# Softmax: the row scale is taken from the probabilities to the attention output, and s is loaded first

## The chip, the cores and the metric

One core of a Trainium2 chip runs the whole program. Its engines work side by side, each through its own list of instructions in a fixed order: TensorE (PE; PEld is its weight load), VectorE (DVE), ScalarE (ACT), GpSimd (POOL), and SyncE (SP), whose queue issues every DMA here. An instruction waits on semaphores of the others, and whatever stands behind it on its engine waits with it. The metric is the device time of one execution in microseconds (us).

## What is computed

```
# 64 heads (8 batches x 8), 576 tokens, 64 columns a head
scores = q @ k.T / 8 - (cum[i] - cum[j])      # cum = cumsum(max(s, 0)), causal
attn = exp(scores - rowmax)
attn = attn / (sum(attn, -1) + 1e-9)
x = attn @ v                                  # 8 heads side by side: 576 x 512 a batch
# then, for each batch, a gated MLP with a token mixing
h = gelu(x @ w_in); u, v = halves of h
v_n = (v - mean) / sqrt(var + 1e-6) * g_ln
out = x + (u * (w_sg @ v_n + b_sg)) @ w_out
```

All of it is in float32; most matrix products are made of two or three products of parts (a high part in float32r and the rest).

## The kernel before, in words

**Attention.** A head goes through three generators. `scores(h)` forms the scores of the 576 rows in five row tiles `it` (64, 128, 128, 128 and 128 rows; because of the causal mask they need 64, 192, 320, 448 and 576 columns). On DVE, `ttr` takes them out of PSUM, adds the mask, and writes them to `pbuf[h % 2][it]` with a running minimum of the negated score in `mn`. `exp_` makes the exponential on ACT in place and leaves the row sums in `sums`. `norm` then takes the reciprocal of the sums (`rs`, one value a row) and multiplies the probabilities by it, in seven pieces, six of them in place or nearly so on POOL for a head below 12 (the 448 columns of tile 3 go to ACT there) and all seven on POOL for the others. Three of the pieces also carry a 64 x 64 block into a free corner of another tile, so that a transpose later takes two blocks in one go. `transposes(h)` transposes `pbuf` on PE into PSUM tiles `pt`, which ACT and DVE take out; `pv(h)` multiplies by v into `xx` and a small tile `x` (`x0` in the code), and ACT and DVE add the result into `xr`, one tile of 128 x 576 for a pair of heads: partitions are the columns of x, the free axis is the tokens.

**Heads.** The first 8 heads load k and q (`kf`, `qf`) as they are; the others load `raw`, split it on ACT and POOL (`k<-raw`), and move the parts into place by five DMAs on SP, of which `k<-k` and `k<-cum` are the last two. Before head 0, the cumulative sums of s are made: load of `st`, three steps on DVE, a product with a triangle `tri` on PE (`cps`), `cf`, and the rows `kf<-cf`. Eight products `wm` that nobody reads keep PE busy until head 0's scores.

**MLP.** `ffn(b)` begins by splitting the four `xr` tiles of a batch on POOL into `xs`, and then runs units v, u, s and o (PE tiles `vm`, `um`, `sm`, `om`). A weight is loaded once, split by ACT, DVE and POOL (`wraw`, `wbits`, `wi`, `wo`, `ws`) during the first 14 heads or so. Tiles of one tag share a ring of buffers; the ring `gt` holds the gated halves that o units read, and the staging of weights in the beginning; the ring `u2` holds u, the outputs `ot` and other small things.

**What sets the order.** The program is recorded as a list of operations, each with a key (its place in a nominal time line of one head a step); `plan` goes through them by a table of costs, takes for each engine the ready operation that can start first, and by key among those, and fixes each engine's order; `emit` writes it out. All lines of the profile therefore name the line of `emit` that issues, L283, and the tiles tell the operations apart. Of the names in the profile, the buffer numbers are left out: `p` is any tile of `pbuf`, `mn` the minima, `k` any tile of k or its parts, `q` likewise.

Of the kernel before, what the change touches and what calls it, by code (L numbers as in the profile page):

```python
# [21 lines left out]
P = 128  # L22
# [3 lines left out]
CH = S // 2  # L26
# [7 lines left out]

TOK = [0, 1, 2, 5, 6, 8, 7, 4, 3]
IT0 = [0, 64, 448, 192, 320]
ITR = [64, 128, 128, 128, 128]
# [11 lines left out]
NP = 12  # L49
U2 = 7  # L50
ENG = {'k': 'sg', 'vs': 'sg', 'xs': 'gg', 'ln': 'sg', 'gt': 'sg', 'w': 'gg', 'ws': 'sv', 'n': 'ggggg', 'n0': 'gggsg', 'ws1': 'g'}
MT = 52.0
# [36 lines left out]
class View:  # L89
# [330 lines left out]
def tile_attn_gmlp(  # L420
# [91 lines left out]
    for i in range(WARM):  # L512
# [14 lines left out]
                            compare_op=ALU.is_ge, fill=NEG)  # L527
    mask2 = const.tile([P, S], BF16, name="mask2")
    nc.vector.memset(mask2, 0.0)
    for r0, c in ((0, 512), (64, 448)):  # L530
        nc.gpsimd.affine_select(out=mask2[r0:r0 + 64, :], in_=mask2[r0:r0 + 64, :], pattern=[[-1, S]], base=c,
                                channel_multiplier=1, compare_op=ALU.is_ge, fill=NEG)
# [8 lines left out]
    for i in range(2):  # L541
        t = const.tile([66, S], F32R, name=f"q2_{i}")
        nc.vector.memset(t[64:66, :].bitcast(F32), 1.0)
        q2.append(t)
        ts_ = []
        for it in range(5):
            t = const.tile([P, PW[it]], F32, name=f"p_{i}_{it}")
            if PW[it] > ITW[it]:
                nc.gpsimd.memset(t[:, ITW[it]:PW[it]], 0.0)
            ts_.append(t)  # L550
        pbuf.append(ts_)
        t = const.tile([P, 5], F32, name=f"sum_{i}")
        nc.vector.memset(t, 1.0)
        sums.append(t)
# [10 lines left out]
    def part(wide, src, hi, lo):  # L565
        n = 256
        if not wide:
            t = moe.tile([P, 2, CH], F32, name="wst", tag="gt", bufs=5)
            t = t.rearrange("p a n -> p (a n)")[:, 0:n]
            nc.sync.dma_start(out=t, in_=src)  # L570
            split(hi, lo, t, nc.scalar, nc.gpsimd)
            return
        raw = moe.tile([P, CH, 2], I32, name="wraw", tag="gt", bufs=5)
        with later():
# [23 lines left out]
    def w_sg_part():  # L598
# [10 lines left out]
        for f in range(2):  # L609
# [7 lines left out]
            t = moe.tile([P, CH], F32, name="wst", tag="u2", bufs=U2)  # L617
            bh = moe.tile([1, 2, CH], F32R, name="bh", tag="gt", bufs=5)
            nc.sync.dma_start(out=t[0:1, :], in_=b_sg.rearrange("(o t) -> o t", o=1)[:, fs])
# [43 lines left out]
    def ttr(h, it, pst, c0, j0, j1, first):  # L663
        d = heads[h]
        r = ITR[it]
        m0 = (576 if it in (2, 4) else 448) - ITW[it] if it else 320
        mn = d["mn"]
        nc.vector.tensor_tensor_reduce(
            out=pbuf[h % 2][it][0:r, j0:j1], in0=pst[0:r, c0:c0 + j1 - j0],
            in1=(mask2 if it in (2, 4) else mask)[0:r, m0 + j0:m0 + j1], scale=-0.125,  # L670
            scalar=3.0e38 if first else mn[0:r, it:it + 1],
            op0=ALU.add, op1=ALU.min, accum_out=mn[0:r, it:it + 1])

    def exp_(h, it):
        d = heads[h]
        r, w = ITR[it], ITW[it]
        p = pbuf[h % 2][it][0:r, 0:w]
        nc.scalar.activation(out=p, in_=p, func=AF.Exp, bias=d["mn"][0:r, it:it + 1], scale=-1.0,
                             accum_out=sums[h % 2][0:r, it:it + 1])

    def norm(h, its, rs):
        c = slice(min(its), max(its) + 1)
        nc.scalar.activation(out=rs[:, c], in_=sums[h % 2][:, c], func=AF.Copy, bias=1e-9)
        nc.vector.reciprocal(out=rs[:, c], in_=rs[:, c])
        for it in its:
            r, w = ITR[it], ITW[it]
            p = pbuf[h % 2][it][0:r, 0:w]
            e = eng("n0" if h < NP else "n")[it]


            o = [(p, p, rs[0:r, it:it + 1])]
            if it == 0:
                o = [(pbuf[h % 2][3][0:64, 384:448], p, rs[0:64, 0:1])]
            elif it == 1:
                o = [(p[:, 0:P], p[:, 0:P], rs[:, 1:2]),
                     (pbuf[h % 2][2][64:P, 256:320], p[64:P, P:192], rs[64:P, 1:2])]
            elif it == 4:
                o = [(p[:, 0:512], p[:, 0:512], rs[:, 4:5]),
                     (pbuf[h % 2][3][0:64, 448:512], p[0:64, 512:S], rs[0:64, 4:5])]
            for po, pi, f in o:  # L700
                if e is nc.scalar:
                    nc.scalar.activation(out=po, in_=pi, func=AF.Copy, scale=f)
                else:
                    e.tensor_scalar(out=po, in0=pi, scalar1=f, scalar2=1.0, op0=ALU.mult, op1=ALU.mult)

    def scores(h):
# [25 lines left out]
        yield 0.6  # L732
        rs = att.tile([P, 5], F32, name="rs", tag="rs")
        norm(h, (3, 0, 2, 1, 4), rs)
        yield 0.1
# [62 lines left out]
    def pv(h):  # L798
# [40 lines left out]
        hs = slice(64 * half, 64 * half + 64)  # L839
        for ps, o, sl in ((x0, slice(0, 64), slice(0, 64)), (xx, slice(0, 512), slice(64, S))):  # L840
            if f32:
                nc.scalar.copy(out=xt[hs, sl], in_=ps[0:64, o])
            else:
                nc.scalar.copy(out=xt[hs, sl], in_=ps[64:128, o])
                nc.vector.tensor_tensor(out=xt[hs, sl], in0=ps[0:64, o], in1=xt[hs, sl], op=ALU.add)
        del heads[h]
        yield 0.5


    def ffn(b):  # L850
# [24 lines left out]
        def v_unit(tt, _):  # L875
# [33 lines left out]
            gelu2(ps[0:r], t, ps[0:r])  # L909
            bs = moe.tile([P, 6], F32, name="bs", tag="bs", bufs=2)  # L910
            mv = moe.tile([P, 2], F32, name="mv", tag="mv", bufs=2)
            rt = moe.tile([P, 4], F32, name="rt", tag="rt", bufs=2)
            nc.vector.bn_stats(out=bs[0:r], in_=ps[0:r])
# [42 lines left out]
        def s_unit(ch, dt):  # L956
# [141 lines left out]
```

## Time and profile before

| | |
|---|---|
| time, median of 3 runs | 835.5 us (834.99 to 836.14) |
| profiled execution, first to last instruction | 835.4 us, no other time of it is given |
| instructions | 16823 |
| busy: PE, PEld | 795.3 us (95%), 688.4 us (82%) |
| busy: DVE, ACT, POOL | 607.0 us (73%), 581.9 us (70%), 607.3 us (73%) |
| DMA | 69805 packets, 89.30 MB, 107 GB/s over the span |
| mean granted clock of TensorE | 0.994 |

The program starts with the load of s and the cumulative sums (to about 12 us), goes on with the first 12 heads, beside which the weights are loaded and split (to about 160 us), then runs attention of one batch beside the MLP of the one before (to about 760 us), and ends with the MLP of the last batch. A row of grouped instructions reads: engine, operation, out<-in tiles, shape, xcount, then busy us and mean ns of one, then the engine's idle time just before them and what ended it. A row of waits reads: who waited for whom, us in total, times, longest.

### The profile page before, as it was taken

What the parts mean: (1) busy time and instruction counts of PE and PEld (TensorE: products, weight loads), DVE (VectorE), ACT (ScalarE), POOL (GpSimd) and SP (SyncE); (2) the same over time, 40 slices, a digit from 0 to 9 for tenths busy, and PEclk for the clock granted to TensorE, in tenths of its full rate; (3) what the DMA queues carried; (4) which work ended last, traced back from release to release, by engine and by line L of the source; (5) the groups of instructions that cost most, each with busy time, mean ns of one, the idle gap of its engine ahead of it and who ended that gap; (6) DMA issues with size and microseconds to landing.
All of it is one profiled execution on the core that took longest, in us unless ns stands there. A gap on an engine that the chain in (4) does not pass through costs nothing.

```text
span 835.4 us, 16823 instructions
## 1 busy us (share of the span) xinstructions
PE 795.3 (95%) x5097; PEld 688.4 (82%) x5097; DVE 607.0 (73%) x1846; ACT 581.9 (70%) x1620; POOL 607.3 (73%) x1043
## 2 busy tenths in 40 slices
PE   5989888999999999999999999999999999999998
PEld 3445555899888999889988989889988999889998
DVE  4677687866788667986789667886679767984562
ACT  3677787676778577985788666976679766883350
POOL 3786979578587976978677967769769885866351
PEclk9999999999999999999999999999999999999999
DMA  5555653325443444335543435244534354320101
GB/s 184 160 172 168 160 129 96 97 75 148 114 102 84 119 124 118 92 87 136 127 108 74 119 106 146 54 112 119 132 82 108 92 139 117 94 46 22 49 7 57
DMA packets 69805, 89.30 MB, mean 107 GB/s; under 512 B 25954, under 2 KB 42212, under 8 KB 69716
## 3 DMA queue, kind: packets, MB, share of 16 engines
q1 hardware_dynamic: 69716, 88.23, 40.2%
q8 instruction: 41, 0.67, 0.4%
q14 instruction: 48, 0.39, 0.2%
HBM read 42.27 MB, written 9.73 MB: 62 GB/s over the span
## 4 chain that ended last, share of the span: by engine, by line
PE 75%; DVE 7%; ACT 6%; POOL 6%; DMA 2%; issue 2%; SPq 0%; POOLq 0%; DVEq 0%; ACTq 0%
PE sm L283 13%; PE om L283 12%; PE xx L283 11%; PE sc L283 10%; PE vm L283 10%; PE pt L283 9%; PE um L283 9%; POOL p L283 3%; ACT p L283 2%; DVE p L283 1%; DMA raw<-in_kq 1%; DVE vt L283 1%; DVE u L283 1%; PE x L283 1%; ACT xr L283 1%
## 5 line engine op out<-in xcount | busy, mean ns | idle before, releaser
L283 POOL TENSOR_SCALAR p<-p,rs 128x512 f32<-128x512 f32 (+3 forms) x436 | 194.5, 457 | 37.7 <-DVE rs L283 22.5
L283 ACT ACTIVATE p<-p,mn 128x448 f32<-128x448 f32 (+4 forms) x320 | 177.8, 557 | 37.2 <-DVE mn L283 35.7
L283 PE MATMUL pt<-ident,p 128*128 128x128 f32 x768 | 154.4, 283 | 10.5 <-POOL p L283 5.0
L283 DVE CUSTOM_DVE_ANT_0 p<-sc,mask 128x448 f32<-128x448 f32 (+4 forms) x320 | 124.6, 419 | 32.8 <-PE sc L283 23.8
L283 PE MATMUL sc<-k,q 66*128 66x288 f32 (+9 forms) x672 | 142.2, 313 | 4.0 <-DVE mn L283 2.0
L283 PE MATMUL um<-xs,wi 128*128 128x288 f32 x768 | 135.6, 305 | 3.1 <-DVE vt L283 2.3
L283 PE MATMUL sm<-ws,vn 128*128 128x288 f32 x768 | 135.5, 305 | 1.2 <-DVE u L283 1.0
L283 PE MATMUL om<-gt,wo 128*128 128x288 f32 x768 | 132.4, 301 | 0.0
L283 PEld LDWEIGHTS pt<-ident,p 128*128 128x128 f32 x768 | 95.5, 141 | 39.7 <-POOL p L283 12.2
L283 PE MATMUL vm<-wi,xs 128*128 128x512 f32 (+1 forms) x416 | 124.6, 407 | 0.0
L283 PEld LDWEIGHTS um<-xs,wi 128*128 128x128 f32 x768 | 113.0, 190 | 7.0 <-DVE vt L283 4.1
L283 PEld LDWEIGHTS sm<-ws,vn 128*128 128x128 f32 x768 | 112.9, 190 | 4.3 <-DVE u L283 3.5
L283 PEld LDWEIGHTS sc<-k,q 128*128 128x128 f32 (+3 forms) x672 | 102.3, 183 | 16.1 <-DVE mn L283 4.5
L283 PEld LDWEIGHTS om<-gt,wo 128*128 128x128 f32 x768 | 112.3, 189 | 2.1 <-POOL gt L283 0.2
L283 POOL TENSOR_TENSOR k<-raw,k 128x576 fp32r<-128x576 f32 x56 | 80.2, 1432 | 36.2 <-ACT k L283 36.2
L283 PEld LDWEIGHTS vm<-wi,xs 128*128 128x128 f32 (+1 forms) x416 | 72.8, 185 | 11.4 <-POOL xs L283 0.2
L283 POOL TENSOR_TENSOR gt<-u,gt 128x288 fp32r<-128x288 f32 x64 | 50.6, 805 | 32.3 <-ACT gt L283 32.1
L283 POOL TENSOR_TENSOR vs<-vr,vs 128x384 fp32r<-128x384 f32 x52 | 52.6, 1011 | 27.5 <-ACT vs L283 26.0
L283 DVE SCALAR_TENSOR_TENSOR u<-u,um 128x288 f32<-128x288 f32 x128 | 56.4, 443 | 14.3 <-ACT u L283 13.4
L283 DVE TENSOR_TENSOR pbl<-pt,pbh 128x512 fp32r<-128x512 f32 x104 | 56.6, 549 | 8.8 <-ACT pbh L283 8.4
L283 ACT CAST pbh<-pt 128x512 fp32r<-128x512 f32 x104 | 49.5, 481 | 17.1 <-PE pt L283 16.8
L283 ACT ACTIVATION_READ_ACCUMULATOR p<-p,mn 128x1 f32 (+1 forms) x320 | 60.4, 189 | 0.0
(122 smaller groups left out, 1547.0 us busy)
## 6 DMA issues: line engine op xcount, KB each, us to landing
q<-k SPq DMA_DIRECT2D x168, 144.0 KB
raw<-in_kq SPq DMA_DIRECT2D x56, 288.0 KB
vr<-in_vp SPq DMA_DIRECT2D x52, 192.0 KB
out_t<-ot SPq DMA_DIRECT2D x64, 144.0 KB
k<-k SPq DMA_DIRECT2D x56, 144.0 KB
wraw<-in_w_in SPq DMA_DIRECT2D x16, 256.0 KB
kf<-in_kq SPq DMA_DIRECT2D x8, 288.0 KB
qf<-in_kq SPq DMA_DIRECT2D x8, 288.0 KB
```

The source lines that it names most:

```text
L283: r = getattr(op["eng"].real, op["name"])(*[f(a) for a in op["args"]], **{k: f(v) for k, v in op["kw"].items()})
```

## The change

`norm` goes, and with it the multiplication of the probabilities. The transposes take the bare exponentials. Two pieces that `norm` had moved while it scaled them are now plain copies of 64 x 64 on POOL (the 64 x 64 tile 0 is exponentiated by ACT right into its corner of tile 3, out of another corner of the same tile, where DVE puts it). The row scale is needed along the free axis now, since `xr` has the tokens there: the reciprocals `rs`, 128 x 5, go to a row `rd` in memory, one element of 4 bytes at a time, and are read back into 64 partitions at once (`rb`, 64 x 576 for each head of a pair). After the second head of a pair, POOL multiplies `xr` by `rb`, 128 x 576. So that `rd` is in the order of the tokens in `xr`, the order of the token blocks changes (`TOK`, `IT0`, and `COL`, the column of the sums). `rb` has one buffer; to make room for it the mask is cut to what is used and the ring `gt` goes from 5 buffers to 4, while `u2` goes from 7 to 8. The operations of the beginning get the key -5, ahead of all loads.

```diff
-TOK = [0, 1, 2, 5, 6, 8, 7, 4, 3]
-IT0 = [0, 64, 448, 192, 320]
+TOK = [1, 2, 5, 6, 8, 7, 4, 3, 0]
+IT0 = [512, 0, 384, 128, 256]
+COL = [4, 0, 3, 1, 2]
...
-U2 = 7
+U2 = 8
...
+    nc.key = -5.0
     dram = Pool(ctx.enter_context(tc.tile_pool(name="dram", bufs=1, space=bass.MemoryType.DRAM)), "dram", 1, dram=True)
...
-        raw = moe.tile([P, CH, 2], I32, name="wraw", tag="gt", bufs=5)
+        raw = moe.tile([P, CH, 2], I32, name="wraw", tag="gt", bufs=4)
...
     def exp_(h, it):
...
-        nc.scalar.activation(out=p, in_=p, func=AF.Exp, bias=d["mn"][0:r, it:it + 1], scale=-1.0,
-                             accum_out=sums[h % 2][0:r, it:it + 1])
-
-    def norm(h, its, rs):
...
-            for po, pi, f in o:
-                if e is nc.scalar:
-                    nc.scalar.activation(out=po, in_=pi, func=AF.Copy, scale=f)
-                else:
-                    e.tensor_scalar(out=po, in0=pi, scalar1=f, scalar2=1.0, op0=ALU.mult, op1=ALU.mult)
+        nc.scalar.activation(out=p if it else pb[3][0:64, 384:448], in_=p, func=AF.Exp,
+                             bias=d["mn"][0:r, it:it + 1], scale=-1.0,
+                             accum_out=sums[h % 2][0:r, COL[it]:COL[it] + 1])
+        for po, pi in {1: [(pb[2][64:P, 256:320], p[64:P, P:192])],
+                       4: [(pb[3][0:64, 448:512], p[0:64, 512:S])]}.get(it, []):
+            nc.gpsimd.tensor_scalar(out=po, in0=pi, scalar1=1.0, scalar2=1.0, op0=ALU.mult, op1=ALU.mult)
+
+    scale_rows = {}
+
+    def scales(h):
+        rs = att.tile([P, 5], F32, name="rs", tag="rs")
+        nc.scalar.activation(out=rs, in_=sums[h % 2], func=AF.Copy, bias=1e-9)
+        nc.vector.reciprocal(out=rs, in_=rs)
+        rd = dram.tile([1, 5 * P], F32, name="rd", tag="rd", bufs=4)
+        nc.sync.dma_start(out=rd.rearrange("o (c p) -> p (o c)", p=P), in_=rs)
+        if h % 2 == 0:
+            scale_rows[h // 2] = att.tile([P, S], F32, name="rb", tag="rb", bufs=1)
+        hs = 64 * (h % 2)
+        nc.sync.dma_start(out=scale_rows[h // 2][hs:hs + 64, :], in_=rd[:, 0:S].spread(64))
...
     def scores(h):
...
-        rs = att.tile([P, 5], F32, name="rs", tag="rs")
-        norm(h, (3, 0, 2, 1, 4), rs)
+        scales(h)
...
     def pv(h):
...
+        if half:
+            nc.gpsimd.tensor_tensor(out=xt, in0=xt, in1=scale_rows.pop(h // 2), op=ALU.mult)
...
-            t = moe.tile([P, 2, CH], F32R, name="gt", tag="gt", bufs=5)
+            t = moe.tile([P, 2, CH], F32R, name="gt", tag="gt", bufs=4)
```

Since `plan` sets the order, the change moves more than the lines of the diff. Three places:

SP, the first rows of its queue, before and then after:

```order
L283 DMA kf<-in_kq 128x576
L283 DMA qf<-in_kq 128x576
L283 DMA vf<-in_vp 128x6x64
L283 DMA st<-in_s_t 128x320
L283 DMA kf<-in_kq 128x576
```

```order
L287 DMA st<-in_s_t 128x320
L287 DMA kf<-in_kq 128x576
L287 DMA qf<-in_kq 128x576
L287 DMA vf<-in_vp 128x6x64
L287 DMA kf<-in_kq 128x576
```

The load of `st` stood behind three loads of head 0 and is now in front of them; the rest keeps its order.

PE, from the last scores of head 0 (`sc`) on, before and then after (`p_3_127`, `p_2_125` and `p_1_199` are tiles 3, 2 and 1 of the buffer of even heads):

```order
L283 MATMUL sc<-kf,qf 128x288 x2
L283 MATMUL sc<-kf,qf 128x448
L283 MATMUL sc<-kf,qf 64x64
L283 MATMUL sc<-kf,qf 128x320
L283 MATMUL sc<-kf,qf 128x192
L283 MATMUL sc<-kf,qf 128x288 x2
L283 MATMUL pt<-ident,p_3_127 128x128
L283 MATMUL pt<-ident,p_2_125 128x128
```

```order
L287 MATMUL sc<-kf,qf 128x288 x2
L287 MATMUL pt<-ident,p_3_127 128x128 x3
L287 MATMUL sc<-kf,qf 128x448
L287 MATMUL pt<-ident,p_2_125 128x128
L287 MATMUL sc<-kf,qf 64x64
L287 MATMUL sc<-kf,qf 128x320
L287 MATMUL pt<-ident,p_1_199 128x128
L287 MATMUL pt<-ident,p_2_125 128x128
```

The transposes of head 0 stood behind all the scores of head 1 and now stand among them.

SP, in the middle of the program, the five DMAs that set up one head, before and then after (`k1`, `k2`, `q1`, `q2` are the parts of k and q; the numbers are those of the buffers):

```order
L283 DMA q1_5531<-k1_5518 64x576
L283 DMA q2_0_93<-k1_5518 64x576
L283 DMA out_t<-ot_5537 128x288
L283 DMA raw_5559<-in_kq 128x576
L283 DMA q1_5531<-k2_5533 64x576
L283 DMA xq_5595<-xs_5007 128x2x64
L283 DMA xq_5595<-xs_5020 128x2x64
L283 DMA k1_5518<-k1_5518 64x576
L283 DMA k2_5533<-cum_175 2x576
```

```order
L287 DMA rd_5916<-rs_5900 128x5x1
L287 DMA q1_5923<-k1_5902 64x576
L287 DMA q2_0_90<-k1_5902 64x576
L287 DMA raw_5954<-in_kq 128x576
L287 DMA q1_5923<-k2_5930 64x576
L287 DMA rb_5973<-rd_5916 64x576
L287 DMA k1_5902<-k1_5902 64x576
L287 DMA k2_5930<-cum_175 2x576
```

The write of `rd` and the read of `rb` stand among them now, `rb` four rows behind `rd` and ahead of the last two DMAs of the head's set-up.

More of the change, by code (lines that the diff above doesn't have):

```diff
@@ L49 @@
 NP = 12
-U2 = 7
-ENG = {'k': 'sg', 'vs': 'sg', 'xs': 'gg', 'ln': 'sg', 'gt': 'sg', 'w': 'gg', 'ws': 'sv', 'n': 'ggggg', 'n0': 'gggsg', 'ws1': 'g'}
+U2 = 8
+ENG = {'k': 'sg', 'vs': 'sg', 'xs': 'gg', 'ln': 'sg', 'gt': 'sg', 'w': 'gg', 'ws': 'sv', 'ws1': 'g'}
 MT = 52.0
@@ L114, in rearrange, with spread @@
         return self.step(dims, self.off, lambda x: x.rearrange(text, **kw))
+    def spread(self, rows):
+        return self.step([(0, rows)] + self.dims[1:], self.off, lambda x: x.broadcast_to([rows, x.shape[1]]))
     def bitcast(self, dt):
@@ L527, in tile_attn_gmlp @@
                             compare_op=ALU.is_ge, fill=NEG)
-    mask2 = const.tile([P, S], BF16, name="mask2")
+    mask2 = const.tile([P, 320], BF16, name="mask2")
     nc.vector.memset(mask2, 0.0)
-    for r0, c in ((0, 512), (64, 448)):
-        nc.gpsimd.affine_select(out=mask2[r0:r0 + 64, :], in_=mask2[r0:r0 + 64, :], pattern=[[-1, S]], base=c,
+    for r0, c in ((0, 256), (64, 192)):
+        nc.gpsimd.affine_select(out=mask2[r0:r0 + 64, :], in_=mask2[r0:r0 + 64, :], pattern=[[-1, 320]], base=c,
                                 channel_multiplier=1, compare_op=ALU.is_ge, fill=NEG)
@@ L544, in tile_attn_gmlp @@
         q2.append(t)
-        ts_ = []
-        for it in range(5):
+        ts_ = [None]
+        for it in range(1, 5):
             t = const.tile([P, PW[it]], F32, name=f"p_{i}_{it}")
@@ L567, in part @@
         if not wide:
-            t = moe.tile([P, 2, CH], F32, name="wst", tag="gt", bufs=5)
+            t = moe.tile([P, 2, CH], F32, name="wst", tag="gt", bufs=4)
             t = t.rearrange("p a n -> p (a n)")[:, 0:n]
@@ L617, in w_sg_part @@
             t = moe.tile([P, CH], F32, name="wst", tag="u2", bufs=U2)
-            bh = moe.tile([1, 2, CH], F32R, name="bh", tag="gt", bufs=5)
+            bh = moe.tile([1, 2, CH], F32R, name="bh", tag="gt", bufs=4)
             nc.sync.dma_start(out=t[0:1, :], in_=b_sg.rearrange("(o t) -> o t", o=1)[:, fs])
@@ L665, in ttr @@
         r = ITR[it]
-        m0 = (576 if it in (2, 4) else 448) - ITW[it] if it else 320
+        m, m0 = (mask2, 320) if it in (2, 4) and j1 == ITW[it] else (mask, 448)
+        m0 = 0 if j1 < ITW[it] else m0 - ITW[it] if it else 320
         mn = d["mn"]
         nc.vector.tensor_tensor_reduce(
-            out=pbuf[h % 2][it][0:r, j0:j1], in0=pst[0:r, c0:c0 + j1 - j0],
-            in1=(mask2 if it in (2, 4) else mask)[0:r, m0 + j0:m0 + j1], scale=-0.125,
+            out=pbuf[h % 2][it][0:r, j0:j1] if it else pbuf[h % 2][3][0:64, 448:512], in0=pst[0:r, c0:c0 + j1 - j0],
+            in1=m[0:r, m0 + j0:m0 + j1], scale=-0.125,
             scalar=3.0e38 if first else mn[0:r, it:it + 1],
@@ L676, in exp_ @@
         r, w = ITR[it], ITW[it]
-        p = pbuf[h % 2][it][0:r, 0:w]
-        nc.scalar.activation(out=p, in_=p, func=AF.Exp, bias=d["mn"][0:r, it:it + 1], scale=-1.0,
-                             accum_out=sums[h % 2][0:r, it:it + 1])
-    def norm(h, its, rs):
[L682 to L699, printed above, removed]
-            for po, pi, f in o:
-                if e is nc.scalar:
-                    nc.scalar.activation(out=po, in_=pi, func=AF.Copy, scale=f)
-                else:
-                    e.tensor_scalar(out=po, in0=pi, scalar1=f, scalar2=1.0, op0=ALU.mult, op1=ALU.mult)
@@ new lines, in exp_ @@
+        pb = pbuf[h % 2]
+        p = pb[it][0:r, 0:w] if it else pb[3][0:64, 448:512]
+        nc.scalar.activation(out=p if it else pb[3][0:64, 384:448], in_=p, func=AF.Exp,
[4 more added lines that the diff above has]
+            nc.gpsimd.tensor_scalar(out=po, in0=pi, scalar1=1.0, scalar2=1.0, op0=ALU.mult, op1=ALU.mult)
@@ L839, in pv @@
         hs = slice(64 * half, 64 * half + 64)
-        for ps, o, sl in ((x0, slice(0, 64), slice(0, 64)), (xx, slice(0, 512), slice(64, S))):
+        for ps, o, sl in ((x0, slice(0, 64), slice(512, S)), (xx, slice(0, 512), slice(0, 512))):
             if f32:
@@ L909, in v_unit @@
             gelu2(ps[0:r], t, ps[0:r])
-            bs = moe.tile([P, 6], F32, name="bs", tag="bs", bufs=2)
-            mv = moe.tile([P, 2], F32, name="mv", tag="mv", bufs=2)
-            rt = moe.tile([P, 4], F32, name="rt", tag="rt", bufs=2)
+            bs = moe.tile([P, 12], F32, name="bs", tag="bs", bufs=2)
+            bs, mv, rt = bs[:, 0:6], bs[:, 6:8], bs[:, 8:12]
             nc.vector.bn_stats(out=bs[0:r], in_=ps[0:r])
```

## Prediction

> **What bounds the kernel now.** I read the totals first, then the windows, to see where PE is not busy; then what PE waited for; last the chain of work that ended last, which tells what lay behind those waits.
>
> ```profile
> span 835.4 us, 16823 instructions
> PE 795.3 (95%) x5097; PEld 688.4 (82%) x5097; DVE 607.0 (73%) x1846; ACT 581.9 (70%) x1620; POOL 607.3 (73%) x1043
> ```
> ```profile
> core 0: us, PE busy (x) PEld busy (x) DVE busy (x) ACT busy (x) POOL busy (x), PEclk, DMA share, GB/s
> 0.00:12.00 12.00, 3.48 (x11) 3.12 (x12) 4.60 (x14) 2.47 (x4) 3.88 (x14) 1.00 0.49 145
> 12.00:160.00 148.00, 131.86 (x626) 81.74 (x625) 105.13 (x331) 109.04 (x319) 117.43 (x195) 0.98 0.53 147
> 160.00:700.00 540.00, 529.34 (x3574) 481.12 (x3573) 412.44 (x1277) 401.99 (x1122) 412.51 (x699) 1.00 0.43 110
> 700.00:836.00 136.00, 130.62 (x892) 122.39 (x890) 84.81 (x226) 68.44 (x177) 73.45 (x136) 1.00 0.18 49
> ```
>
> PE is the bound, and it is idle for only 40 us: 8.5 at the start (12 - 3.48), 16.1 in the first heads (148 - 131.86), 10.7 in the long middle (540 - 529.34), and about 5 behind that. The middle cannot give much. In the first heads, POOL is next in load (117.43 of 148, 79%).
>
> ```profile
> PE pt L283 <- POOL p L283: 5.0, 12, 1.0
> PE sc L283 <- DVE mn L283: 4.3, 5, 1.8
> PE pt L283 <- ACT pah L283: 3.5, 5, 1.1
> PE sc L283 <- DMA k<-cum: 1.5, 1, 1.5
> ```
>
> Only 5.0 us are laid to the step that goes (`pt` waits for POOL's `p`). The same waits counted for the first heads and for the middle:
>
> ```profile
> PE pt L283 <- POOL p L283: 2.6, 6, 1.0
> ...
> PE pt L283 <- POOL p L283: 2.0, 5, 0.8
> ```
>
> The chain shows more of it, since POOL's `p` also holds up DVE and ACT, for which PE waits later. First the chain from 12 to 160, then from 160 to 700:
>
> ```profile
> by line: PE xx L283 18.6%; PE sc L283 13.5%; POOL p L283 8.4%; PE pt L283 7.8%; ACT p L283 4.6%; issue 4.4%; DMA raw<-in_kq 3.9%; PE vm L283 3.6%; DVE p L283 3.3%; DVE wbits L283 3.1%; DVE vt L283 2.8%; POOL wi L283 2.4%; PE um L283 2.3%; P
> ...
> by line: PE sm L283 14.7%; PE om L283 13.4%; PE pt L283 11.3%; PE sc L283 11.2%; PE vm L283 11.1%; PE xx L283 10.6%; PE um L283 9.5%; issue 1.7%; POOL p L283 1.5%; DVE vt L283 1.2%; ACT p L283 1.1%; DMA raw<-in_kq 0.9%; PE x L283 0.9%; DVE
> ```
>
> POOL's `p` is 8.4% of 148 us = 12.4 us of the chain in the first heads, and 1.5% of 540 = 8.1 us in the middle.
>
> **The change, part by part.** The start first.
>
> ```profile
> 0.78 0.39 SPq L283 DMA_DIRECT2D kf<-in_kq  x1
> 2.41 0.63 SPq L283 DMA_DIRECT2D st<-in_s_t  x1
> 3.38 0.48 DVE L283 MEMSET vnr<- 2x512 f32 x1
> 7.00 0.33 DVE L283 TENSOR_SCALAR st<-st 128x320 f32<-128x320 f32 x1 [3.14 <-DMA st<-in_s_t]
> 8.52 2.56 PE L283 MATMUL cps<-tri,sp 128*128 128x512 f32 x9 [8.52 <-DVE sp L283]
> 11.00 3.78 PE L283 MATMUL wm<-tri,sp 128*128 128x512 f32 x8
> 14.58 1.70 PE L283 MATMUL sc<-kf,qf 128*128 128x448 f32 x2
> ```
> ```profile
> 2.00:3.00 1.00, 0.00 (x0) 0.00 (x0) 0.80 (x3) 0.06 (x1) 1.00 (x3) 1.00 0.97 293
> ```
>
> `st` is issued at 2.41 and used at 7.00: 4.6 us, with 768 KB of head 0 ahead of it at 293 GB/s (2.6 us) and 0.16 MB of its own. In front of them it is issued at 0.78, 1.63 us earlier, and is alone. DVE is free from 3.86 on, so the gain is at most 7.00 - 3.86 = 3.1, and at least 1.6 (the earlier issue alone). I take 2.8, near the upper end, because 1.63 + 2.6 is more than DVE can use. Everything to the scores at 14.58 follows on PE without a gap (8.52 + 2.56, 11.00 + 3.78), so it moves as a whole; `kf` and `qf` come 0.63 us later, hidden by the 10 us until they are used. **Start: -2.8.**
>
> Now `norm`. Its pieces, and the two-input product on POOL that is nearest to the new one on `xr`:
>
> ```profile
> L283 POOL TENSOR_SCALAR p<-p,rs 64x64 f32<-64x64 f32 x192 | 61.6, 321 | 6.5 <-ACT p L283 0.3
> L283 POOL TENSOR_SCALAR p<-p,rs 128x512 f32<-128x512 f32 x64 | 44.9, 701 | 5.4
> L283 POOL TENSOR_SCALAR p<-p,rs 128x320 f32<-128x320 f32 x64 | 35.1, 549 | 2.8 <-DVE wbits L283 2.4 <-DVE rs L283 0.4
> L283 POOL TENSOR_SCALAR p<-p,rs 128x448 f32<-128x448 f32 x52 | 33.7, 648 | 22.9 <-DVE rs L283 22.1 <-DVE mn L283 0.6
> L283 POOL TENSOR_SCALAR p<-p,rs 128x128 f32<-128x128 f32 x64 | 24.0, 375 | 0.0
> L283 POOL TENSOR_TENSOR k<-raw,k 128x576 fp32r<-128x576 f32 x56 | 80.2, 1432 | 36.2 <-ACT k L283 36.2
> L283 ACT ACTIVATE p<-p,rs 128x448 f32<-128x448 f32 x12 | 8.1, 671 | 1.1 <-DVE rs L283 1.0
> ```
>
> A head paid POOL 3 x 321 + 701 + 549 + 648 + 375 = 3236 ns; two copies of 321 remain, 642, a fifth. With the multiplication of `xr`, 32 x 1432 ns = 45.8 us, and 128 x 321 = 41.1 us of copies, POOL does 87 us where it did 194.5: its total goes from 607 to 500. ACT loses 8.1 us. What counts is the path. In the first heads, four fifths of 12.4 = 9.9 us leave the chain at most; at least the 2.6 that PE waited for POOL's `p` itself. Between the two DVE (`mn`) and ACT (`pah`) are late next, so I take the middle, 6.2. PE idles 16.1 there, so there is room. The moved transposes of head 0 belong to this: they need no more than the exponentials. **First heads: -6.2.** In the middle the ends are 8.1 x 0.8 = 6.5 and 2.0; PE is 98% busy there, so I stay near the wait: **-2.5.**
>
> Added: per head one write of `rd` (640 elements of 4 bytes) and one read of `rb` (144 KB), 128 DMAs in all on SP.
>
> ```profile
> q1 hardware_dynamic: 69716, 88.23, 40.2%
> ...
> 104.41 5.76 DMA raw<-in_kq
> ...
> SPq L283 <- DMA q<-k: 100.4, 58, 3.7
> 420.26 0.18 DVE L283 RECIPROCAL rs<-rs 128x5 f32<-128x5 f32 x1
> 431.74 0.22 DVE L283 TENSOR_TENSOR xr<-x,xr 64x64 f32<-64x64 f32 x1
> ```
>
> No row shows a packet of 4 bytes that carries data. A mean packet (1266 bytes) takes 0.402 x 16 x 835.4 us / 69716 = 77 ns, so 640 of them on 16 engines take between nothing and 3.1 us, a head. One DMA lands in between 1.7 us (100.4 / 58, what SP waited for `q<-k`) and 5.8 us (`raw`); the round trip is 3.5 to 11.5. From the reciprocal to the first add into `xr` there are 11.5 us in the middle, so the trip is hidden, the more since the product comes only behind the second head of the pair; without that cover each pair would wait for the rest, up to 3 us. What it can hold up is SP: behind `rb` stand `k<-k` and `k<-cum`. I take 0 in the middle; ends: 0, and the rival below. The multiplication itself stands ahead of POOL's `xs` split. In the first batch that split is on the chain, and there I charge one multiplication, 1.4 (ends 0 and 4 pairs x 1.43 = 5.7). The smaller ring `gt` and the order of tokens: 0.1, hidden by PE's work on other heads. **Added: +1.5.**
>
> The end of the program:
>
> ```profile
> 759.45 0.27 PE L283 MATMUL x<-pdh,vs 128*128 128x64 f32 x1
> 771.82 1.56 PE L283 MATMUL vm<-wi,xs 128*128 128x512 f32 x6
> 822.40 9.67 PE L283 MATMUL om<-gt,wo 128*128 128x288 f32 x72
> 825.15 2.34 POOL L283 TENSOR_TENSOR gt<-u,gt 128x288 fp32r<-128x288 f32 x3 [9.10 <-ACT gt L283]
> ```
>
> Between the last product of head 63 and the first `vm` of the last batch lie 12 us of other matmuls, which cover the last multiplication and its round trip. With four `gt` buffers, four splits instead of three come late, 0.78 us more on POOL (2.34 / 3), under 9.67 us of matmuls that PE can still pick from. I take **-0.3**, for the last of the waits on POOL's `p`.
>
> Sum: -2.8 - 6.2 - 2.5 + 1.5 - 0.3 = -10.3. Against the span of 835.4, that is 825.1; the median of the runs is 0.1 above that span, so I say **825 us** (-1.3%).
>
> The Trainium skill has a rule against this change: its page "DMA: Bandwidth & Descriptors", section "Rules for kernel authors", says that a pattern whose last dimension is not contiguous becomes one descriptor per element, and advises to rearrange it; section "Specifications" adds that below 512 bytes the engine reads, modifies and writes. `rd` is such a pattern. By that page's fit (section "Anatomy of one DMA", about 2.0 us + bytes / 436e3, for DMAs that GpSimd issues) the two DMAs would take an estimated 2.0 + 2.3 = 4.3 us, inside the 3.5 to 11.5 above, and the sum would not change.
>
> **The rivals.** (1) *Only the visible waits go.* PE, freed from POOL's `p`, meets DVE's `mn` or ACT's `pah` a moment later: -2.8 - 2.6 - 2.0 with the added 1.5 and a late `rb` in the first heads, another 1.5: 831. For it: DVE is 71% busy in the first heads, and the waits on `mn` and `pah` (7.8 us) are larger than those on `p`. Against: the 12.4 us of the chain.
>
> (2) *More than the visible idle.* Busy PE is not PE at its peak. If the waits of its weight loads go too, the ends of both ranges are reached: -2.8 - 9.9 - 6.5 + 0.5 = -18.7, 816.7; since the durations within PE's busy time would shrink with it, I say 815. For it:
>
> ```profile
> L283 PEld LDWEIGHTS pt<-ident,p 128*128 128x128 f32 x768 | 95.5, 141 | 39.7 <-POOL p L283 12.2 <-ACT pah L283 5.2 <-issue 3.4
> ```
>
> 12.2 us of PEld's idle time were ended by POOL's `p`, over twice PE's own 5.0. Against: PE had other matmuls queued for most of them. The Trainium skill, page "Perfetto Trace Analysis", section "Identifying the Most-Contended Engine", states this rival as a rule: matmul busy time is a bad measure of the distance to the bound, weight-load busy time a good one; by it 82% is the figure.
>
> (3) *Slower: SP's queue.* `rb` waits for `rd` to land and for the last pair's multiplication to free the one buffer; `k<-k` and `k<-cum` stand behind it, and the scores of the next head wait for them. Before, this showed once, 1.5 us. If one head in four of the 56 pays it, that is 14 x 1.5 = 21 us, and the time 846. It decides from 10.3 / 56 = 0.18 us a head on. Against: `rb` stands four DMAs behind `rd`, and a head's split has a key 0.4 steps ahead of its scores (`POS`).
>
> **How the numbers follow.** My forecast (819 to 831) gets 0.58, (1) 0.17, (2) 0.12, (3) 0.13. A change of 0.2%, 1.7 us, is about what a measurement can tell here. (1) reaches from 830 up to no change; I count 0.07 of it as same, and 0.01 of (3). So faster 0.80, same 0.08, slower 0.12. The range 814 to 835 reaches to (1) and (2) and leaves out (3) and the far ends of those two, some 0.2; my forecast's own is 819 to 831.
>
> **What would show it.** `cps` starts at about 5.7; no `pt <- POOL p` wait above 0.5 us; POOL busy near 500 us; PE idle in the first heads near 10 us, and near 8 in the middle; DMA share a few points higher. Wrong, if PE waits for `k<-cum` or `k<-k` in many heads, if POOL waits for `rb` ahead of `k<-raw` or `xs`, or if the idle time of the first heads stays at 16 under another name.

## The result, and the profile after

The changed kernel takes 1114.7 us (median of 4 runs, 1109.3 to 1121.8) where the kernel before took 835.7 beside it (834.99 to 836.14): ratio 1.334, 95% interval 1.328 to 1.340. The forecast was 825, with a range of 814 to 835. The profiled execution has a span of 1110.1 us and a mean granted clock of 0.891 (before: 0.994).

The totals of the page after, then the windows:

```profile
span 1110.1 us, 16781 instructions
PE 879.0 (79%) x5097; PEld 752.0 (68%) x5097; DVE 608.9 (55%) x1846; ACT 579.1 (52%) x1608; POOL 490.1 (44%) x767
DMA packets 116909, 98.91 MB, mean 89 GB/s; under 512 B 68962, under 2 KB 85220, under 8 KB 116820
q1 hardware_dynamic: 116820, 97.84, 60.5%
```
```profile
0.00:12.00 12.00, 6.42 (x18) 5.29 (x19) 4.78 (x14) 2.74 (x4) 4.85 (x15) 1.00 0.55 161
12.00:160.00 148.00, 105.04 (x403) 58.10 (x402) 66.34 (x223) 67.49 (x210) 60.50 (x82) 0.80 0.78 123
160.00:700.00 540.00, 431.29 (x2598) 383.71 (x2597) 310.55 (x953) 303.44 (x840) 248.15 (x382) 0.90 0.66 91
1000.00:1111.00 111.00, 96.28 (x644) 91.35 (x643) 50.50 (x120) 35.60 (x86) 41.16 (x70) 0.94 0.11 31
```

POOL fell from 607 to 490 us (500 was forecast), and PE runs the same 5097 matmuls. But PE now stands idle for 231 us (1110.1 - 879.0) where it was 40, and is busy 84 us longer at a lower granted clock, all along the program. The packets of the DMA engines take 60.5% of a span that is a third longer (40.2% before), with only 11% more bytes and 68% more packets (116820 against 69716). The chain of work that ended last, by engine and by line, says what it is:

```profile
DMA 53%; PE 21%; issue 7%; ACT 7%; POOL 5%; DVE 4%; SPq 3%; POOLq 0%; ACTq 0%; DVEq 0%
DMA rd<-rs 19%; DMA q<-k 8%; DMA raw<-in_kq 6%; PE sm L287 6%; DMA rb<-rd 5%; DMA vr<-in_vp 4%; DMA k<-k 4%; PE om L287 3%; SPq L287 3%; PE sc L287 3%; ACT p L287 3%; PE pt L287 2%; DMA vnr<-vnr 2%; DMA wraw<-in_w_in 2%; PE vm L287 2%
```

Pieces of that chain in order of time (start, us, what; a DMA counts from its issue to its landing), and SP's timeline around one of them:

```profile
45.82 10.90 DMA rd<-rs
121.46 9.10 DMA rd<-rs
130.63 7.47 DMA rb<-rd
420.72 11.16 DMA q<-k
437.77 11.06 DMA rd<-rs
```
```profile
402.60 0.58 SPq L287 DMA_DIRECT2D rd<-rs  x1
403.28 0.54 SPq L287 DMA_DIRECT2D q<-k  x1
403.86 0.58 SPq L287 DMA_DIRECT2D raw<-in_kq  x1
404.49 0.47 SPq L287 DMA_DIRECT2D q<-k  x1
405.43 0.34 SPq L287 DMA_DIRECT2D out_t<-ot  x1
413.50 0.47 SPq L287 DMA_DIRECT2D rb<-rd  x1
```

On the chain the 2.5 KB of `rd` need 9 to 11 us to land (20 of its 21 pieces among the longest of the chain; one took 15.3), nearly as long as the 11.5 us that were to hide the whole round trip. SP stands in front of `rb` from 405.8 to 413.5. An ordinary `q<-k` of 144 KB takes up to 11 us as well, where a `raw` of twice the size took 5.8 us before. The waits, of SP's queue and then of the engines:

```profile
SPq L287 <- DMA rd<-rs: 319.3, 57, 9.0
SPq L287 <- DMA q<-k: 117.5, 56, 6.6
```
```profile
PE pt L287 <- ACT p L287: 89.0, 23, 6.0
PE pt L287 <- POOL p L287: 27.3, 7, 6.0
PE sc L287 <- DMA k<-k: 17.6, 7, 3.3
POOL xr L287 <- DMA rb<-rd: 83.7, 13, 12.8
```

SP waits for `rd` 57 times, 5.6 us each on average. PE's own largest wait names `ACT p`. One piece of the chain shows how a late `rd` gets to PE:

```profile
457.32 10.95 DMA rd<-rs
468.91 3.04 DMA k<-k
472.09 1.25 PE sc L287 x5
```

SP issues `rb` only when `rd` has landed (468.3), `k<-k` behind it, and the scores start when that k is there. Whether each of PE's 23 waits for `ACT p` goes back to a late k, the views do not show.

### The profile page after: what moved, and what is told of

The parts are those of the page before. It is cut to its first block, busy times and chain, and to the rows that moved or that the text cites. A ratio compares the mean times of both kernels' runs of the same rounds, so it can differ in the third digit from the quotient of the medians.

```text
span 1110.1 us, 16781 instructions
## 1 busy us (share of the span) xinstructions
PE 879.0 (79%) x5097; PEld 752.0 (68%) x5097; DVE 608.9 (55%) x1846; ACT 579.1 (52%) x1608; POOL 490.1 (44%) x767
## 2 busy tenths in 40 slices
DMA packets 116909, 98.91 MB, mean 89 GB/s; under 512 B 68962, under 2 KB 85220, under 8 KB 116820
## 3 DMA queue, kind: packets, MB, share of 16 engines
q1 hardware_dynamic: 116820, 97.84, 60.5%
## 4 chain that ended last, share of the span: by engine, by line
DMA 53%; PE 21%; issue 7%; ACT 7%; POOL 5%; DVE 4%; SPq 3%; POOLq 0%; ACTq 0%; DVEq 0%
DMA rd<-rs 19%; DMA q<-k 8%; DMA raw<-in_kq 6%; PE sm L287 6%; DMA rb<-rd 5%; DMA vr<-in_vp 4%; DMA k<-k 4%; PE om L287 3%; SPq L287 3%; PE sc L287 3%; ACT p L287 3%; PE pt L287 2%; DMA vnr<-vnr 2%; DMA wraw<-in_w_in 2%; PE vm L287 2%
## 5 line engine op out<-in xcount | busy, mean ns | idle before, releaser
L287 PE MATMUL pt<-ident,p 128*128 128x128 f32 x768 | 180.2, 313 | 135.0 <-ACT p L287 89.0
L287 PEld LDWEIGHTS pt<-ident,p 128*128 128x128 f32 x768 | 109.5, 157 | 174.5 <-ACT p L287 98.8
L287 ACT ACTIVATE p<-p,mn 128x320 f32<-128x320 f32 (+4 forms) x320 | 177.3, 555 | 20.0 <-DVE mn L287 19.0
L287 PE MATMUL sc<-k,q 66*128 66x288 f32 (+9 forms) x672 | 144.9, 324 | 44.9 <-DMA k<-k 17.6
L287 PE MATMUL sm<-ws,vn 128*128 128x288 f32 x768 | 153.9, 330 | 1.3 <-DVE u L287 1.3
L287 PE MATMUL om<-gt,wo 128*128 128x288 f32 x768 | 140.3, 322 | 5.0 <-POOL gt L287 5.0
L287 PE MATMUL vm<-wi,xs 128*128 128x512 f32 (+1 forms) x416 | 141.5, 445 | 0.0
L287 PEld LDWEIGHTS sm<-ws,vn 128*128 128x128 f32 x768 | 129.2, 213 | 4.8 <-DVE u L287 2.9
L287 POOL TENSOR_TENSOR xr<-xr,rb 128x576 f32<-128x576 f32 x32 | 46.0, 1437 | 130.2 <-DMA rb<-rd 83.7
L287 PEld LDWEIGHTS vm<-wi,xs 128*128 128x128 f32 (+1 forms) x416 | 78.9, 206 | 11.1 <-issue 1.0
L287 ACT CAST k<-raw 128x576 fp32r<-128x576 f32 x56 | 37.3, 667 | 74.4 <-DMA raw<-in_kq 27.3
L287 DVE TENSOR_TENSOR pbl<-pt,pbh 128x512 fp32r<-128x512 f32 x104 | 56.9, 552 | 29.4 <-ACT pbh L287 28.8
```

The lines of the kernel that those rows point to most:

```text
L287: r = getattr(op["eng"].real, op["name"])(*[f(a) for a in op["args"]], **{k: f(v) for k, v in op["kw"].items()})
```

## The experiments

Three theories stood for the loss. *Engines*: the 640 separate elements of `rd` occupy the DMA engines, so the transfers behind them are late, whether anyone waits for `rd` or not. *Queue* (the prediction's third rival): SP stands in front of `rb` and holds up the loads behind it. *Rest*: the forecast gains were wrong too. In the first kernel the order of every engine is that of the changed kernel. The next two were planned anew: `rb`, which need not wait there, moves ahead of `rd` on SP, the two of a pair side by side, and the orders of PE, DVE, ACT and POOL change too.

**One write in runs.** The partition is the slow index, 128 runs of 20 bytes; the scale values meet wrong tokens.

```diff
-        nc.sync.dma_start(out=rd.rearrange("o (c p) -> p (o c)", p=P), in_=rs)
+        nc.sync.dma_start(out=rd.rearrange("o (p c) -> p (o c)", c=5), in_=rs)
```

> The changed kernel with rd laid out the other way round: each partition writes its 5 values as one run of 20 bytes, 128 runs for 640 single elements; the read of rb and every engine's order stay as they are (the values of the scale go to the wrong tokens). If the single elements are what costs (one piece of work for each), the write falls from about 9 us to 2 or 3 us, rb no longer waits, and the time comes to the forecast, 820 to 835 us. If a write to memory of less than 512 bytes is slow whatever its length, or if it is the round trip as such, little changes: above 1000 us.

Measured: 828.0 us (826.8 to 830.0), ratio 0.987 (0.984 to 0.990). The same bytes, the same wait of `rb` for `rd`, the same order: the loss is gone, and the total comes within 3 us of the forecast.

**The wait taken away.** `rd` is written element by element as in the changed kernel, but `rb` reads a row of `cum`, so nobody waits for `rd`; the scale is left out.

```diff
-        nc.sync.dma_start(out=scale_rows[h // 2][hs:hs + 64, :], in_=rd[:, 0:S].spread(64))
+        nc.sync.dma_start(out=scale_rows[h // 2][hs:hs + 64, :], in_=cum[0:1, h, :].spread(64))
```

> The changed kernel with rd written as before, element by element, but rb read from a row of cum that has lain in memory since the start (the scale is left out); so nothing on SP waits for rd by need. Theory 'queue order' (SP stands still at rb until rd has landed, and the set-up of heads behind it comes late): 820 to 840 us. Theory 'DMA engines' (the elements keep the 16 engines busy for about 9 us a head, so that every transfer behind them is late): still above 950 us.

**The write taken away too.** As the last, without the write of `rd`.

> No write of rd at all; rb is read from a row of cum that is ready (the scale is left out). Everything else of the change is there: the transposes without the scaling, POOL's product on xr, 64 reads of rb, the ring gt of 4, s first. If the write of rd is the whole loss: 820 to 830 us, as forecast. If POOL's product, the smaller ring or the new order cost too: above 835 us.

Measured: unread 1050.6 us (ratio 1.252, 1.246 to 1.258), unwritten 823.8 (0.982, 0.979 to 0.985). So of the 290.9 us between the changed kernel and the one without the write, 226.8 us (1050.6 - 823.8), or 3.5 us a head, are lost with nobody waiting for `rd`. The other 64.1 us (1114.7 - 1050.6) lie between two kernels that differ in the wait and in their orders, so they are no clean price of the wait. *Rest* falls: without the write the time is even below the forecast. The waits of SP's queue with `rd` unread, and the DMA queue in the two kernels, unread and unwritten:

```profile
SPq L287 <- DMA q<-k: 401.9, 84, 10.6
SPq L287 <- DMA rd<-rs: 24.7, 9, 5.2
```
```profile
q1 hardware_dynamic: 116820, 97.84, 59.3%
```
```profile
q1 hardware_dynamic: 74836, 97.67, 44.8%
```

With the wait for `rd` gone, SP's time goes to `q<-k`, up to 10.6 us (3.7 before): ordinary transfers that stand behind the elements. That the elements delay others with nobody waiting is the main part; *queue* is about a fifth of the loss, if the new order neither costs nor gains.

**Only the load of s.** The kernel before with the key -5 for its first operations, planned anew.

```diff
+    nc.key = -5.0
     dram = Pool(ctx.enter_context(tc.tile_pool(name="dram", bufs=1, space=bass.MemoryType.DRAM)), "dram", 1, dram=True)
```

> The kernel before with only the key of the beginning set to -5, so that s is loaded first. My step for the start: cps begins 2.8 us earlier and all that follows moves with it, 832.7 us. The rival: the first heads wait for something else (weights, POOL), and 1 us or less is left, 834.5 us or more.

Measured: 839.0 us (836.4 to 840.6), ratio 1.001 (0.999 to 1.003). `cps` starts at 5.55 instead of 8.52, and the end gains nothing. The same move with every other order left alone:

```diff
+    first_load = [nc.sync.dma_start(out=st, in_=s_t)]
...
+    i = first_load[0]          # the load of st
+    seqs[SP].remove(i)
+    seqs[SP].insert(0, i)
+    start[i] = -1.0
```

> The kernel before, with the load of s put first in SP's queue by hand and every other order as it was, on all engines; the run with the key alone had planned everything anew and gained 0 (1.0013). Theory 'start is worth its 2.9 us': cps starts 2.9 us earlier and the end comes 2.5 to 3 us earlier, ratio 0.9965 to 0.997. Rival 'swallowed': the heads behind catch on the loads of k and q and of the weights, which do not come earlier, and the end moves by less than 1 us: 0.999 to 1.0.

Measured: 833.8 us (831.6 to 835.5), ratio 0.996 (0.995 to 0.998). PE's first products, in this kernel:

```profile
5.55 2.55 PE L283 MATMUL cps<-tri,sp 128*128 128x512 f32 x9 [5.55 <-DVE sp L283]
```

About 3 us are gained where nothing else moves (2.0 to 4.4 us by the interval); the new plan for the kernel before lost them again. This is the only complete kernel of the study that beats the kernel before.

**What it is about the elements that costs.** The next kernels write `rd` unread, the scale left out, with the order of the unread kernel on every engine. They differ in where the elements go or in how many there are (`dims` stands for `[(1, P), (1, 5)]`): the five elements of a partition 8 bytes apart in a block of 64 bytes of their own; all elements 512 bytes apart; one column of 128 adjacent elements:

```diff
+        rd = dram.tile([1, 16 * P], F32, name="rd", tag="rd", bufs=4)         # own block
+        rv = rd.step(dims, rd.off, lambda x: x.rearrange("o (p c t) -> p (o c) t", p=P, t=2)[:, 0:5, 0])
---
+        rd = dram.tile([1, 5 * P * 128], F32, name="rd", tag="rd", bufs=4)    # 512 apart
+        rv = rd.step(dims, rd.off, lambda x: x.rearrange("o (c p t) -> p (o c) t", p=P, t=128)[:, :, 0])
---
+        rv = rd.step(dims, rd.off, lambda x: x[:, 0:P].rearrange("o (c p) -> p (o c)", p=P))  # one column
+        nc.sync.dma_start(out=rv, in_=rs[:, 0:1])
```

> As the run with rd unread (640 single elements of 4 bytes, rb from a row of cum, the scale left out), but the five elements of one partition lie 8 bytes apart in a block of 64 bytes of their own; every engine's order is that of the unread run. Theory 'count' (each single element costs the DMA engines the same wherever it goes): 1040 to 1060. Rival 'shared blocks' (neighbouring elements of one block of memory, written from different partitions and by different engines, wait for each other): the elements of one block come from one partition now, so most of the 227 us goes: 825 to 870.

> As the run with rd unread (640 single elements of 4 bytes, the scale left out), but each element lies 512 bytes from the next, so no two share a block of memory; same order on every engine. Theory 'count': 1040 to 1060. Rival 'shared blocks': 825 to 870; if this and the run with 64-byte blocks differ, the size of the block lies between 64 and 512 bytes, or the way in which a partition's elements are spread over engines decides.

> As the run with rd unread, but one column only is written: 128 single elements of 4 bytes at adjacent addresses (the scale left out); same order on every engine. Theory 'count', in proportion: a fifth of 227 us, so about 824 + 45 = 869. Count with slack in the engines (the first pieces are hidden, as 128 runs of 20 bytes were): 825 to 835. Rival 'shared blocks', in which neighbouring elements wait for each other: 869 too, or more, while the run with 512 bytes between elements is at 825 to 870.

Measured: 842.4 us, 821.9 and 964.7. *Count* falls: the same 640 elements cost nothing that can be seen at 512 bytes apart, and a fifth of them, adjacent, cost 141 us (964.7 - 823.8). The DMA queue at 512 bytes apart has the packets of the changed kernel, and a share near that of the unwritten one:

```profile
q1 hardware_dynamic: 116820, 97.84, 47.1%
```

Then the spacing (the tile `rd` grows with it in each):

```diff
+        rv = rd.step(dims, rd.off, lambda x: x.rearrange("o (c p t) -> p (o c) t", p=P, t=16)[:, :, 0])  # 64 apart
+        rv = rd.step(dims, rd.off, lambda x: x.rearrange("o (c p t) -> p (o c) t", p=P, t=2)[:, :, 0])   # 8 apart
+        rv = rd.step(dims, rd.off, lambda x: x[:, 8:8 + 10 * P].rearrange("o (c p t) -> p (o c) t", p=P, t=2)[:, :, 0])  # 32 on
```

> As the run with elements 512 bytes apart (640 single elements, rd unread, the scale left out; same order on every engine), but 64 bytes apart: eight elements in 512 bytes, one in 64. Theory 'block of at most 64 bytes': 820 to 826, as with 512. Rival 'block of 512 bytes', in which eight writes from eight partitions meet: 835 to 900.

> As the run with rd unread, but the elements lie 8 bytes apart in the same order (column by column): 8 elements in 64 bytes, where adjacent ones are 16 (1050.6) and the run with a block for each partition had 5 (842.4). Theory 'number of writes in a 64-byte block', between these two points: 870 to 960. Rival 'different engines': if consecutive eighths of the partitions go to the 16 DMA engines, eight elements of one column 8 bytes apart fill one block from one engine alone, and only a block written by two engines costs: 825 to 845.

> As the run with elements 8 bytes apart (854.1; rd unread, the scale left out; same order on every engine), but all of it 32 bytes further on in memory. If consecutive eighths of the partitions go to the 16 DMA engines, each block of 64 bytes then holds four elements from one engine and four from the next, where before all eight were of one. Theory 'number of writes in a block': no change, 850 to 858. Rival 'a block shared by two engines costs more' (which would explain the jump from 854 with eight in a block to 1050 with sixteen): above 880.

Measured: 821.6 us, 854.1 and 851.6. With the runs above:

| elements written a head | elements in 64 bytes | us | above unwritten (823.8) |
|---|---|---|---|
| 640, 512 apart | 1 | 821.9 | -1.9 |
| 640, 64 apart | 1 | 821.6 | -2.2 |
| 640, a block for each partition | 5 | 842.4 | 18.6 |
| 640, 8 apart | 8 | 854.1 | 30.3 |
| 640, 8 apart, 32 further | 8 | 851.6 | 27.8 |
| 640, adjacent | 16 | 1050.6 | 226.8 |
| 128, adjacent | 16 | 964.7 | 140.9 |

Each of these ran two to four times, and the kernel before took 836.4 to 837.7 us beside them, so differences of about 2 us say nothing. An element that has 64 bytes of memory to itself is free here; with five or eight in 64 bytes it costs a little, with sixteen much. The cleanest pair is 64 bytes apart against adjacent: the same packets in the same order, 821.6 us against 1050.6.

The packet records of these two traces say where the time goes. The 4-byte packets themselves take about 9 ns each in both, in sum 27.8 and 28.8 us for each of the 16 engines. The packets of 2304 bytes, the rows of transfers such as `raw`, `q<-k` and `rb`, take 244 us for each engine in one and 443 in the other; the longest is 1.3 us in one and 8.7 in the other. So *engines* is right that other transfers are late, but not because the elements fill the engines: their own packets are short, and it is the packets of others that grow.

What in the neighbourhood costs is open. Eight in 64 bytes came out below the 870 to 960 that the number of writes was to give and above the 825 to 845 of its rival, and at sixteen the cost jumps sevenfold, which no run explains. Nor does it follow the number of elements: 640 adjacent ones cost 227 us, 128 cost 141. The run moved by 32 bytes tests the rival of a block shared by two engines only if an engine takes eight neighbouring partitions, as its expectation supposes, and if a block is 64 bytes. If an engine takes four, both runs have two engines in each 64 bytes, and the adjacent elements have four. Which elements went to which engine is not in the trace, so this rival stands untested. Nor is the size of a block known: only the spacing was varied.

**A mended kernel.** The whole computation, with fewer pieces. First 128 runs of 16 bytes and 64 single elements, then 64 runs of 20 bytes and 64 of 16; both need a second DMA a head and two products on POOL instead of one, strided ones but for the last 64 tokens of the first kernel. Both are planned anew (the comment at the end stands for the code of the products):

```diff
+        nc.sync.dma_start(out=rd[:, 0:512].rearrange("o (p c) -> p (o c)", c=4), in_=rs[:, 0:4])
+        nc.sync.dma_start(out=rd[:, 512:S].rearrange("o (c p) -> p (o c)", p=REM), in_=rs[0:REM, 4:5])
---
+        nc.sync.dma_start(out=rd[:, 0:320].rearrange("o (p c) -> p (o c)", c=5), in_=rs[0:64, :])
+        nc.sync.dma_start(out=rd[:, 320:S].rearrange("o (p c) -> p (o c)", c=4), in_=rs[64:P, 0:4])
+        # POOL: xr[:, c, p] * rb[:, (p c)], 5 x 64 tokens and 4 x 64
```

> The whole computation, with the scale. rd is written with the partition as the slow index: 128 runs of 16 bytes for four row tiles and 64 single elements for the fifth, 192 pieces a head where the changed kernel writes 640; one DMA more a head on SP; POOL multiplies the 512 tokens in one step through a strided view of rb and the last 64 in another. Theory 'pieces' (a head's loss lies in the 640 pieces of rd's write): the 128 runs of 20 bytes cost 4 us over the unwritten rd, so 192 pieces cost about 6, and the DMA and POOL's second product some 2: 828 to 833, faster than before by 0.6 to 1.1%. Rival 'order' (what saved the run with 20-byte runs was that nothing but the write changed): the order is planned anew here, and the re-planned start gained nothing: 834 to 842.

> The whole computation, with the scale. rd is 576 elements, written in two DMAs: from partitions 0 to 63 all five columns, 64 runs of 20 bytes, and from partitions 64 to 127 four columns, 64 runs of 16 bytes; no single elements are left. POOL multiplies in two steps with strided views (5 x 64 and 4 x 64 tokens). Theory 'shared blocks' (it is the number of separate writes into one small block of memory that costs): about 4 writes fall into 64 bytes here, as in the run with 20-byte runs (828.0), where the run with 16-byte runs and 64 single adjacent elements had 16 of the latter in 64 bytes (971.5): 825 to 834, faster than before by 0.4 to 1.4%. Rival 'partition-major runs of under 20 bytes cost too' (the 16-byte runs, not the 64 single elements, made that run slow): above 880.

Measured: 971.5 us (ratio 1.160, 1.156 to 1.164) and 842.2 (1.007, 1.004 to 1.009), both outside what either side expected. Only 64 adjacent single elements were left in the first, sixteen in 64 bytes, and it is 129 us slower than the second; runs of 16 bytes are in both. But the second is not at 828 either. Its own order, or the second write and product?

> The whole computation, with the scale: the two writes of rd with runs of 20 and 16 bytes and the two products on POOL as in the run before with those runs (842.2), but every engine's order is that of the changed kernel; the second write and the second product only follow their first. Theory 'new order' (what that run lost against the run with 20-byte runs alone, 828.0, came with the order that was planned anew): 827 to 833, faster than before by 0.5 to 1.2%. Rival 'the writes' (its 64-partition writes give each DMA engine 80 bytes, so that two engines meet in most blocks of 64 bytes, and the second write and product cost the rest): 838 to 845.

Measured: 844.0 us (ratio 1.009, 1.006 to 1.012): not the order. Then each half by itself, in that order (scale values on wrong tokens):

> The order of the changed kernel, rd in two writes (64 runs of 20 bytes and 64 of 16), but one plain product on POOL as in the changed kernel (the scale values meet wrong tokens). With one write of 128 runs and one product it was 0.9868 of the kernel before (828.0), with two of each 1.0088 (844.0). Theory 'second write' (a further DMA a head on SP's queue, whose issue and landing delay what stands behind): 838 to 846. Rival 'second product' (POOL's two strided products, 1.9 us a pair where one plain product took 1.4): 826 to 832.

> The other half: one write of 128 runs of 20 bytes, and two strided products on POOL (the scale values meet wrong tokens). Theory 'second write': 826 to 832. Rival 'second product': 838 to 846. If both kernels are near 836, both cost.

Measured: 833.3 us (ratio 0.996, 0.994 to 0.998) and 834.8 (0.997, 0.995 to 0.999). Against 0.987 with one of each, the second write costs 0.9% (7.6 us) and the second product 1.0% (8.4 us); both together 2.2%. The first expected one culprit; the second allowed for two, and both cost something. The groups of POOL's product with one write of 20-byte runs and one product, then with two writes, then with two strided products (this last row counts both, 128x320 and 128x256):

```profile
L287 POOL TENSOR_TENSOR xr<-xr,rb 128x576 f32<-128x576 f32 x32 | 45.7, 1429 | 16.8 <-DMA rb<-rd 7.5 <-DVE mn L287 4.2 <-ACT p L287 2.6
```

```profile
L287 POOL TENSOR_TENSOR xr<-xr,rb 128x576 f32<-128x576 f32 x32 | 45.8, 1431 | 23.8 <-DMA rb<-rd 12.1 <-DVE mn L287 6.2 <-ACT rs L287 3.1
```
```profile
L287 POOL TENSOR_TENSOR xr<-xr,rb 128x320 f32<-128x320 f32 x64 | 60.2, 962 | 15.4 <-DMA rb<-rd 13.2 <-DVE xr L287 1.0 <-DVE mn L287 0.3
```

The strided pair takes 1.92 us (2 x 962) where the plain product took 1.43, and with either change POOL waits 12 to 13 us for `rb` instead of 7.5. That fits the direction; how these few microseconds grow to 8 in each case the runs do not show.

## Why the prediction was wrong

**The step that failed is the term *Added*, +1.5.** It took the write of `rd` as a delay of its own: "so 640 of them on 16 engines take between nothing and 3.1 us, a head", hidden behind the 11.5 us until the first add into `xr`, so 0 in the middle. What the write can hold up on SP it took as 0, and for what it does to other transfers it had no term. The elements' own packets stayed inside that bound: with them the 4-byte packets take 28.8 us for each engine, without them 5.8, which is 0.36 us a head. But with nobody waiting for `rd` at all, the adjacent elements cost 229.0 us, 3.6 a head, against the same elements 64 bytes apart (1050.6 - 821.6), because ordinary transfers came late. The trip was not hidden either: `rd` alone takes 9 to 11 us, and one round trip of the chain 16.6 (121.46 to 138.10), where 3.5 to 11.5 was put. The low end of that came from what SP waited for `q<-k`, which is only the part of a landing that SP had to stand through. The sentence ahead of the sum, "No row shows a packet of 4 bytes that carries data", was the warning; the range should have stayed open upward there. Why close elements hold up others stays open.

**The third rival had the direction and a part of the mechanism.** It named SP's queue with `rb` in front of `k<-k`, and priced it at 21 us; the piece of the chain from 457.32 on is just that. But the wait for `rd` is about 64 us of the loss, if the new order neither costs nor gains; the larger part, 227 us, comes with nobody waiting for `rd`. The sign of it that the prediction would watch for, "if PE waits for `k<-cum` or `k<-k` in many heads", shows only eleven times (`k<-k` 7 times, 17.6 us, and `k<-cum` 4 times, 3.7 us); the largest wait of PE is that for `ACT p`.

**The Trainium skill's rule, named in the prediction, was given no chance of its own.** Page "DMA: Bandwidth & Descriptors", section "Rules for kernel authors": an access pattern whose last dimension isn't contiguous becomes one descriptor per element. The trace agrees: with the write there are 41,984 packets more than without (116820 - 74836), 656 a head for 640 elements. The fit from that page, an estimated 4.3 us for both DMAs, is far from 9 to 11 us for the first of them. The section "Specifications" of that page says that below 512 bytes the engine reads, modifies and writes; measured, 640 writes of 4 bytes cost nothing that can be seen when 64 bytes apart (821.6 us against 823.8 without them), so it is not the size of a write alone that costs here but how close together they lie.

**The other terms held in the kernel without the write, and less well with one.** The windows of the kernel without the write, which is planned anew and leaves out the scale:

```profile
0.00:12.00 12.00, 6.41 (x19) 5.07 (x19) 4.79 (x14) 2.75 (x4) 4.87 (x15) 1.00 0.56 161
12.00:160.00 148.00, 135.75 (x685) 89.09 (x685) 114.58 (x357) 110.03 (x330) 101.59 (x148) 0.97 0.62 169
160.00:700.00 540.00, 531.30 (x3608) 488.12 (x3607) 418.99 (x1287) 406.24 (x1129) 328.84 (x500) 1.00 0.47 123
```
```profile
PE 788.9 (96%) x5097; PEld 690.1 (84%) x5097; DVE 610.8 (74%) x1846; ACT 576.3 (70%) x1608; POOL 493.7 (60%) x767
```

- *Start, -2.8:* PE's idle time falls from 8.5 to 5.6 us, and moving the load alone gave 2.0 to 4.4. Right.
- *First heads, -6.2 (2.6 to 9.9):* idle 16.1 to 12.3, so -3.9. In the range, nearer the wait itself than the chain.
- *Middle, -2.5 (2.0 to 6.5):* idle 10.7 to 8.7, so -2.0. Right, at its low end.
- *What was not in the sum:* PE's busy time fell by 6.4 us (795.3 - 788.9), as the second rival had said it might. The whole change of the span is -15.0 (835.4 - 820.4), more than the -11.8 that the terms without *Added* come to; in medians it is -13.9 (823.8 against 837.7 of the kernel before in the same series).

With one write in runs the sum comes out right in total: 828.0 against 837.7 beside it, -9.7, where -10.3 was forecast. That is partly luck, as its windows show:

```profile
12.00:160.00 148.00, 136.96 (x679) 87.96 (x678) 115.17 (x356) 110.28 (x330) 101.13 (x149) 0.95 0.68 168
160.00:700.00 540.00, 527.07 (x3574) 483.51 (x3574) 415.32 (x1272) 403.74 (x1119) 326.45 (x496) 1.00 0.48 121
```

Idle time falls by 5.1 us in the first heads (16.1 to 11.0), but in the middle it rises by 2.3 (10.66 to 12.93), where -2.5 was forecast; the median is 4.2 us above the kernel without the write, so even a write in runs is not free. And its tokens are not the reference's; the complete kernels give the gain back in the second write and the second product.

## What to carry to other kernels

Before moving a small per-partition vector through memory, look at where neighbouring elements land: here many 4-byte writes into the same 64 bytes delayed ordinary transfers by several microseconds, and neither a mean packet of the trace before nor the length of the 4-byte packets themselves shows that. Give each element 64 bytes of its own (how such a row reads back no run here shows), or write runs; and price also what the mended layout costs (here a second write and a second, strided product, 0.9% and 1.0%), since together that was more than the idea had gained. When a plan is made anew, a gain at the start can be lost behind it: about 3 us here, kept when only the one load was moved.

## What was not expected of the hardware

In the stretches in which PE waits, its clock is lower too: granted 0.80 and 0.90 in the first two long windows of the changed kernel (0.98 and 1.00 before), and the same 5097 matmuls took 84 us more of busy time. The clock is enough for that: if all of it went by the clock, 795.3 x 0.994 / 0.891 is 887 us, and 879.0 were measured. The Trainium skill, page "TensorE: Matmul & The Clock Gate", section "HAM oscillation — how this bites in real kernels", describes this: waits for a DMA let the clock be throttled, and the next stretch starts slow. The trace agrees in that clock and waits go together; that the waits are the cause no run here separates. Of the 275 us by which the span grew (1110.1 - 835.4) the longer busy time is nearly a third.
